# Sink-window attention and two MoE layers: the sinks' columns copied on ScalarE, and the last block split later

## The chip, the cores and the metric

The kernel runs on one core of a Trainium2 chip. The metric is the device time of one launch in microseconds, the median of three runs. TensorE, VectorE, ScalarE, GpSimd and SyncE each work through an instruction queue of their own in order; they wait for one another by semaphores. In the rows below PE is TensorE's matmul side and PEld its weight loads, DVE is VectorE, ACT is ScalarE, POOL is GpSimd, and SP is SyncE, which issues the DMAs.

## The reference

Attention over two batches of 8 heads, 768 positions and 64 columns a head, with a causal window of 128 positions and the first 4 positions as sinks that every query sees; then two dense layers over the 1536 tokens of 512 columns, with 2048 hidden columns each.

```python
keep = is_sink | in_window                       # 4 sinks, 128 positions back
scores = np.where(keep, scores, -1000000000.0)
a = np.exp(scores - np.max(scores, axis=-1, keepdims=True))
a = a / (np.sum(a, axis=-1, keepdims=True) + 1e-09)
x = np.matmul(a, v)                              # then (B, H, S, D) -> (1536, 512)

h = x @ w_in                                     # layer 1
g = (a0 + a1 * h + a2 * h**2 + a3 * h**3) / (1 + abs(b0) * abs(h) + abs(b1) * h**2 + 1e-6)
x = g @ w_out

h = np.maximum(x @ w_in2, 0.0)                   # layer 2
out = h * h @ w_out2
```

## The kernel before

**Attention.** The queries go in 12 blocks `u` of 128 rows (6 for each batch), each in two steps `m`, so there are 24 steps (`NM`) and two more, which finish the last block. A step takes four heads. `scores` (L354, L363) multiplies queries by the keys of the block and of the one before it; VectorE folds the two (L368), adds the mask and takes the row's extreme `nmax` (L375); `expo` (L392) is ScalarE's exponential into `pe`, with the row's sum into `rs`; `trans` (L420) transposes, ScalarE copies the result to `pc` (L432), and GpSimd splits it into two triangles `ph` (L433, L437); `pv` (L453) multiplies by the values into the PSUM bank `O`.

The sinks go another way. Their columns of `pe` (8 for each of 8 heads, 64 in all) are copied to `sr` by `sinks` (L401), for every block but the first of a batch, so ten times; `sums` adds a small constant to `rs` on ScalarE (L408) and writes the reciprocal into `sr` as well (L409, VectorE). `sinks_t` transposes `sr` on TensorE (L413) and copies it to `st` (L415); `sinks_and_sums` multiplies it by the sinks' values and spreads the reciprocal sums (L465, L469), which ScalarE copies to `rb` (L471). `result` (L475) multiplies `O` by `rb` on VectorE into `xf`. `parts_of` then makes two numbers of each: `xh`, rounded by ScalarE (L482), and `xl`, the remainder, by GpSimd (L483). The layers' matmuls work on such pairs.

**Layers.** Weights come as 64-bit numbers in four buffers `wr`; VectorE takes them to 32 bits in three instructions (L240, L246, L252, the steps that `w_until` hands out), by way of the bank `U` in the attention and `O` afterwards, as `conv["tag"]` says; then ScalarE rounds (L273) and GpSimd takes the remainder (L274) in `w_fin`. Some of these steps lie between the attention's.

A layer's steps are written out in `slot(k)`: round and remainder of element k-2 (`act_c`, L653 for `gh` and L654 for `gl`), the function of element k-1 (`act_b`: L638 and L639 on ScalarE, L642 to L646 on VectorE), the first matmuls of element k+1 (`g1`, L592), the first part of the function of element k (`act_a`: L608 to L612 on ScalarE, L613 on GpSimd; the cubic term is L621 on VectorE), the second matmuls of element k-2 (`g2`, L671). Slots 0 and 1 take the last two steps of the attention in their middle, as `mid`. `EARLY` is 2: the loop over the other slots begins there, after the attention's buffers are given back.

The order on every engine is that in which the code issues, without a scheduler. The last block (u = 11) lies in the third of the three chunks of 512 tokens; layer 1 begins with the first chunk.

Of the kernel before, what the change touches and what calls it, by code (L numbers as in the profile page):

```python
# [37 lines left out]
def kernel(  # L38
# [13 lines left out]
    nc = tc.nc  # L52
# [4 lines left out]
    NU = B * NB  # L57
# [119 lines left out]
    conv = {"tag": "U", "on": True}  # L177
# [12 lines left out]
    for j, (kind, m) in enumerate(jobs):  # L190
        n = 1 if kind == "v" else 1 + (wtiles[m][::2] == (0, 0)) if kind == "w" else WS + (m >= LATE)
# [73 lines left out]
    def w_fin():  # L265
        m = wst["fin"]
        if m not in wx or len(spare) <= keep[0] or int(spare[0][1:]) >= len(wpool):
            return
        wst["fin"] += 1
        xf = wx.pop(m).bitcast(F32)  # L270
        tag = spare.pop(0)
        t = wpool[int(tag[1:])].tile([P, 2, DM], F32R, tag=tag, name="w")
        nc.scalar.copy(out=t[:, 0], in_=xf)  # L273
        nc.gpsimd.tensor_tensor(out=t[:, 1], in0=xf, in1=t[:, 0].bitcast(F32), op=ALU.subtract)  # L274
        W[wtiles[m]] = (t[:, 0], t[:, 1], tag)
# [17 lines left out]
    def attention(ap, extra):  # L293
# [51 lines left out]
        def scores(n):  # L345
            u, pr = divmod(n, NPR)
            i = u % NB
            t = ss[n % 2]
            d = [t[:, e] for e in range(2)]
            if i == 0:  # L350
                mask, co, bw = m_0, 0, P
                for e in range(2):
                    s = slice(D * e, D * e + D)
                    nc.tensor.matmul(  # L354
                        d[e][:, 0:P], lhsT=ld[u, "q"][s, pr, :], rhs=keys[s, pr, 0, 0:P], start=True, stop=True
                    )
            else:
                mask, co, bw = (m_1 if i == 1 else m_2), P, BS
                hf = P // 2
                for g in range(2):  # L360
                    for e in range(2):
                        s, r = slice(D * e, D * e + D), slice(hf * g, hf * g + BS + hf)
                        nc.tensor.matmul(  # L363
                            d[e][hf * g:hf * g + hf, r], lhsT=ld[u, "q"][s, pr, hf * g:hf * g + hf],
                            rhs=keys[s, pr, i - 1:i + 1, :].rearrange("p i n -> p (i n)")[:, r],
                            start=True, stop=True,
                        )
                nc.vector.copy_predicated(  # L368
                    out=t[:, :, BS:BS + P], mask=tri.unsqueeze(1).to_broadcast([P, 2, P]), data=t[:, :, 0:P]
                )  # L370
            ns = []
            for e in range(2):
                ix = u * H + 2 * pr + e
                t = ap.tile([P, 160], F32, name="ns", bufs=6)
                nc.vector.tensor_tensor_reduce(  # L375
                    out=t[:, 0:bw], in0=d[e][:, co:co + bw], in1=mask, scale=-scale, scalar=3.0e38,
                    op0=ALU.add, op1=ALU.min, accum_out=nmax[:, ix:ix + 1],
                )
                ns.append(t)
            kps[n] = ns  # L380
# [17 lines left out]
        def sinks(u):  # L398
            t = pe_t.pop(u)
            if u % NB:  # L400
                nc.vector.tensor_copy(  # L401
                    sr[u % 2][:, 0:HS].rearrange("p (r e s) -> p r e s", r=NPR, e=2),
                    t[:, :, :, ROW - BS:ROW - P],
                )
# [74 lines left out]
        def parts_of(u):  # L479
            c, t0 = u // UPC, (u % UPC) * P  # L480
            x, h = f.pop(u), xh[c][:, :, t0:t0 + P]
            nc.scalar.copy(out=h, in_=x)  # L482
            nc.gpsimd.tensor_tensor(out=xl[c][:, :, t0:t0 + P], in0=x, in1=h.bitcast(F32), op=ALU.subtract)  # L483

        NM = NU * NPR // 2
# [28 lines left out]
        def step(m):  # L514
            w_fin()
            nonlocal bd, moe, rest, heads
            n, (u, a) = 2 * m, divmod(m, 2)
            if m < NM:
                scores(n)
            if a == 0 and u >= 1:  # L520
                sinks(u - 1)
                sums(u - 1)
            if m < NM:
                scores(n + 1)
                if n in DENSE:
                    fill(ps_t("T"), DENSE[n])
            if m == 0:
                rest = setup_rest(*next(masks), m_1, m_2, tri)
                next(rest)
                sink_keys(0)  # L530
            if a == 0 and 2 <= u <= NU:
                parts_of(u - 2)
            if m < NM:
                expo(n)
            if m in (1, 2):
                next(rest, None)
            if 0 < m <= NM:
                trans(m - 1)
            if m == 1:
                for t in sr:  # L540
                    nc.gpsimd.memset(t, 0.0)
                bd = diagonal()
                heads = bd.rearrange("p h d -> p (h d)")
                moe = setup_moe()
            if a == 0 and u + 2 < NU:
                load(u + 2)
            if a == 0 and m < NM and u % NB == 0:
                load_sinks(u // NB)
            if m >= 5:
                next(moe, None)  # L550
                next(moe, None)
            if a == 1 and u >= 1:
                sinks_and_sums(u - 1)
            if 1 < m:
                pv(m - 2)
            if m < NM:
                expo(n + 1)
            if a == 0 and u >= 1:
                sinks_t(u - 1)
            if m == NM - 1:  # L560
                g1(0)
            if m < NM and a == 1 and u % NB == 0:
                if u:
                    sink_keys(u)
                sink_values(u // NB, bd)
            extra(m)
            if a == 1 and u >= 1:
                result(u - 1)
            if m == NM + 1:
                parts_of(NU - 1)  # L570

        for m in range(NM):
            step(m)
        for j in range(2):
            slot(j, lambda: step(NM + j))


    def part(L, g):
        return CUTS[L][g:g + 2]
# [20 lines left out]
    def layers(mp, due):  # L600
# [56 lines left out]
        def g2(k):  # L657
            L, g, c, f = steps[k]
            f0, f1 = part(L, g)[0], part(L, g)[1] - 1
            if f == f0:  # L660
                acc[L, g, c] = [t[:, m] for t in [ps_s(), ps_s()] for m in range(2)]
            wo = W[L, f, 1]
            gg = gq.pop(k)
            for m in range(4):
                s = slice(m * P, (m + 1) * P)
                for a, b in ((0, 0), (0, 1), (1, 0)):
                    if L == 0:
                        lh, rh = wo[a][:, s], gg[b]
                    else:
                        lh, rh = gg[a][:, s], wo[b]  # L670
                    nc.tensor.matmul(  # L671
                        acc[L, g, c][m], lhsT=lh, rhs=rh,
                        start=(f == f0 and a + b == 0), stop=(f == f1 and a == 1),
                    )
            if c == NCH - 1:
                w_free((L, f, 1))
            if f == f1:
                done.append((L, g, c))
# [45 lines left out]

        K = len(steps)

        def slot(k, mid=None):
            if 0 <= k - 2:
                act_c(k - 2)
            w_fin()  # L730
            w_fin()
            if 0 <= k - 1 < K:
                act_b(k - 1, lambda: w_until(min(due(k), wst["int"] + 1)))
            if k + 1 < K:
                g1(k + 1)
            if k < K:
                act_a(k)
            if mid:
                cubic(st[k][1], hq[k])
                hq[k] = None  # L740
                mid()
            split_late()
            w_until(due(k))
            if 0 <= k - 2:
                g2(k - 2)
            if k == K + 1:
                finish(0)
                finish(1)
# [253 lines left out]
    EARLY = 2  # L1002
# [19 lines left out]
    slot, slots = layers(mp, due)  # L1022
    with tc.tile_pool(name="ap", bufs=1) as ap:
        NM = NU * NPR // 2

        def extra(m):
            if m == 1:
                for _ in range(NWR):
                    w_load()
            if m % 2:  # L1030
                w_until(min(WS * NA, m - 1))
            if m == NM:
                conv["on"] = False

        attention(ap, extra)
    conv["tag"], conv["on"] = "O", True
    wp2 = main.enter_context(tc.tile_pool(name="wp2", bufs=1))
    wpool += [wp2] * (NW - NA)
    for n in range(EARLY, slots):
        slot(n)  # L1040
        if n == KL + 3 * NF - 3:
            fl = verdict()
# [43 lines left out]
```

## Time and profile before

| what | value |
|---|---|
| median of 3 runs | 624.1 us (623.85 to 624.36) |
| the profiled execution | 624.6 us |
| its span, first to last instruction | 622.9 us |
| TensorE matmul busy | 609.0 us (98%) |
| VectorE, ScalarE, GpSimd busy | 434.4, 355.8, 329.2 us |

The span is what the trace covers; the profiled execution's own time has 1.7 us more around it. A busy TensorE is not TensorE at its peak, since matmuls overlap and their ends are modelled. The attention lasts to about 98 us; from there on the layers run.

### The profile page before, as it was taken

To read this page: it belongs to the slowest core of one execution; us is meant where nothing else is said; L and a number is where in the kernel's file an instruction comes from. 1 tells how busy PE (TensorE), PEld (TensorE's weight loads), DVE (VectorE), ACT (ScalarE), POOL (GpSimd) and SP (SyncE) were. 2 spreads that over 40 slices of the span, in tenths; PEclk is the share of its full clock that TensorE was granted. 3 is DMA by queue.
4 is the path that set the end of the run, shared out by engine and by line. 5 is a ranking of instruction groups with operands and counts; after the bars stand their busy time and mean duration, and the time that the engine had idled before them with its cause. 6 is when DMAs were issued, how large, how long until landed. Compare 5 with 4: busy or idle time off the path is not lost.

```text
span 622.9 us, 9430 instructions
## 1 busy us (share of the span) xinstructions
PE 609.0 (98%) x3317; PEld 491.1 (79%) x3317; DVE 434.4 (70%) x873; ACT 355.8 (57%) x748; POOL 329.2 (53%) x293
## 2 busy tenths in 40 slices
PE   9999999999999999999999999999999999999995
PEld 6666777788888878888888888888888888888884
DVE  5998957989989889877768879598594422441421
ACT  5999977888886877877869543243332222222210
POOL 4567655777776767666857575444352222222221
PEclk9999999999999999999999999999999999999999
DMA  8857411423332333121111447557365355500102
GB/s 232 244 146 214 120 36 35 128 87 93 98 102 78 97 97 101 38 64 35 35 34 35 115 148 256 192 176 234 131 207 198 116 191 168 175 28 1 67 1 73
DMA packets 64231, 72.03 MB, mean 116 GB/s; under 512 B 15280, under 2 KB 55216, under 8 KB 64176
## 3 DMA queue, kind: packets, MB, share of 16 engines
q1 hardware_dynamic: 64032, 71.35, 37.1%
q8 instruction: 28, 0.46, 0.3%
q14 instruction: 27, 0.22, 0.1%
q10 hardware_dynamic: 144, 0.00, 0.0%
HBM read 68.20 MB, written 3.15 MB: 115 GB/s over the span
## 4 chain that ended last, share of the span: by engine, by line
PE 65%; DVE 19%; ACT 11%; issue 2%; DMA 1%; SPq 0%; DVEq 0%; ACTq 0%
PE s L671 30%; PE T L592 23%; PE U L592 7%; DVE t L646 3%; DVE U L644 3%; ACT U L638 2%; ACT U L639 2%; ACT gh L653 2%; ACT w L273 2%; DVE t L642 2%; DVE wx L252 2%; DVE ns L375 1%; DVE O L240 1%; PE O L453 1%; PE s L363 1%
## 5 line engine op out<-in xcount | busy, mean ns | idle before, releaser
L592 PE MATMUL T<-xh,w 128*128 128x512 f32 x640 | 211.0, 391 | 0.5 <-DVE t L621 0.4
L654 POOL TENSOR_TENSOR gl<-g,gh 128x512 fp32r<-128x512 f32 x48 | 62.2, 1295 | 157.9 <-ACT gh L653 157.8
L592 PEld LDWEIGHTS T<-xh,w 128*128 128x128 f32 x640 | 120.2, 188 | 27.9 <-DVE t L621 2.7
L671 PE MATMUL s<-gh,w 128*128 128x512 f32 x384 | 126.0, 389 | 0.0
L592 PE MATMUL T<-xl,w 128*128 128x512 f32 x320 | 124.6, 389 | 0.0
L671 PE MATMUL s<-w,gh 128*128 128x512 f32 x384 | 118.1, 389 | 0.0
L274 POOL TENSOR_TENSOR w<-wx,w 128x512 fp32r<-128x512 f32 x64 | 82.7, 1293 | 7.2 <-ACT w L273 7.2
L654 POOL TENSOR_TENSOR gl<-t,gh 128x512 fp32r<-128x512 f32 x48 | 62.1, 1294 | 44.6 <-ACT gh L653 43.0
L671 PEld LDWEIGHTS s<-gh,w 128*128 128x128 f32 x384 | 72.1, 188 | 15.0
L671 PEld LDWEIGHTS s<-w,gh 128*128 128x128 f32 x384 | 72.0, 188 | 14.9
L613 POOL TENSOR_TENSOR t<-t,ah 128x512 f32<-128x512 f32 x48 | 62.2, 1296 | 37.7 <-ACT t L610 35.8
L653 ACT CAST gh<-g 128x512 fp32r<-128x512 f32 x48 | 29.9, 623 | 81.8 <-PE s L671 74.5
L671 PE MATMUL s<-gl,w 128*128 128x512 f32 x192 | 74.8, 390 | 0.9 <-POOL gl L654 0.9
L671 PE MATMUL s<-w,gl 128*128 128x512 f32 x192 | 74.7, 389 | 0.0
L592 PEld LDWEIGHTS T<-xl,w 128*128 128x128 f32 x320 | 60.1, 188 | 12.2
L653 ACT CAST gh<-t 128x512 fp32r<-128x512 f32 x48 | 29.9, 622 | 46.2 <-DVE t L646 41.9
L642 DVE SCALAR_TENSOR_TENSOR t<-t,U 128x512 f32<-128x512 f32 x48 | 33.0, 687 | 30.1 <-ACT U L639 29.5
L627 DVE TENSOR_TENSOR g<-r,T 128x512 f32<-128x512 f32 x32 | 21.8, 683 | 41.8 <-ACT r L617 41.5
L617 ACT ACTIVATE r<-T 128x512 f32<-128x512 f32 x32 | 19.2, 600 | 53.2 <-PE T L592 53.1
L392 ACT ACTIVATE pe<-ns,nmax 128x136 f32<-128x136 f32 (+1 forms) x96 | 38.3, 400 | 10.0 <-DVE nmax L375 9.6
L671 PEld LDWEIGHTS s<-gl,w 128*128 128x128 f32 x192 | 36.0, 188 | 8.8 <-POOL gl L654 1.4
L273 ACT CAST w<-wx 128x512 fp32r<-128x512 f32 x64 | 39.3, 615 | 6.4 <-DVE wx L252 6.4
(136 smaller groups left out, 1033.4 us busy)
## 6 DMA issues: line engine op xcount, KB each, us to landing
wr<-in_w_in_dram SPq DMA_DIRECT2D x54, 512.0 KB, 3.7
wr<-in_w_out_dram SPq DMA_DIRECT2D x52, 512.0 KB, 3.7
qr<-in_q_dram SPq DMA_DIRECT2D x12, 256.0 KB, 4.1
keys<-in_k_dram SPq DMA_DIRECT2D x12, 256.0 KB, 4.5
vr<-in_v_dram SPq DMA_DIRECT2D x12, 256.0 KB, 5.6
wr<-in_v_dram SPq DMA_DIRECT2D x6, 512.0 KB, 4.3
out_dram<-part SPq DMA_DIRECT2D x12, 256.0 KB, 2.0
vsc<-in_v_dram SPq DMA_DIRECT2D x2, 16.0 KB
```

The lines of the kernel that those rows point to most:

```text
L273: nc.scalar.copy(out=t[:, 0], in_=xf)
L274: nc.gpsimd.tensor_tensor(out=t[:, 1], in0=xf, in1=t[:, 0].bitcast(F32), op=ALU.subtract)
L392: nc.scalar.activation(out=t[:, e, ROW - w:], in_=ns[e][:, 0:w], func=ACTF.Exp, scale=-1.0, bias=nmax[:, ix:ix + 1], accum_out=rs[:, 2 * p ...
L592: nc.tensor.matmul(h, lhsT=wi[a][:, kk * P:(kk + 1) * P], rhs=(xh, xl)[b][c][:, kk, :], start=(kk == 0 and a + b == 0), stop=(kk == KD - 1 ...
L613: nc.gpsimd.tensor_tensor(out=t, in0=t, in1=ah, op=ALU.mult)
L617: nc.scalar.activation(out=r, in_=h, func=ACTF.Relu)
L627: nc.vector.tensor_tensor(out=g, in0=st.pop(k), in1=h, op=ALU.mult)
L642: nc.vector.scalar_tensor_tensor(out=t, in0=t, scalar=QP, in1=r0, op0=ALU.add, op1=ALU.mult)
L644: nc.vector.scalar_tensor_tensor(out=r0, in0=t, scalar=-2.0, in1=r0, op0=ALU.add, op1=ALU.mult)
L653: nc.scalar.copy(out=gh, in_=g)
L654: nc.gpsimd.tensor_tensor(out=gl, in0=g, in1=gh.bitcast(F32), op=ALU.subtract)
L671: nc.tensor.matmul(acc[L, g, c][m], lhsT=lh, rhs=rh, start=(f == f0 and a + b == 0), stop=(f == f1 and a == 1),)
```

## The change

`sinks` copies on ScalarE instead of VectorE. In slot 1, `step(NM + 1)` no longer ends with `parts_of(NU - 1)`; slot 2 is taken out of the loop and issued at the end of the attention, and it issues `parts_of(NU - 1)` behind its own `g2`. The bank that the weight steps use is switched one step earlier in the code.

```diff
         def sinks(u):
             t = pe_t.pop(u)
             if u % NB:
-                nc.vector.tensor_copy(
+                nc.scalar.copy(
                     sr[u % 2][:, 0:HS].rearrange("p (r e s) -> p r e s", r=NPR, e=2),
                     t[:, :, :, ROW - BS:ROW - P],
                 )
...
             if a == 1 and u >= 1:
                 result(u - 1)
-            if m == NM + 1:
-                parts_of(NU - 1)
...
         for j in range(2):
             slot(j, lambda: step(NM + j))
+        slot(2, after=lambda: parts_of(NU - 1))
...
-        def slot(k, mid=None):
+        def slot(k, mid=None, after=None):
...
             if 0 <= k - 2:
                 g2(k - 2)
+            if after:
+                after()
...
             if m == NM:
                 conv["on"] = False
+            if m == NM + 1:
+                conv["tag"], conv["on"] = "O", True
 
         attention(ap, extra)
-    conv["tag"], conv["on"] = "O", True
...
-    for n in range(EARLY, slots):
+    for n in range(EARLY + 1, slots):
```

On VectorE, in each of ten blocks of the attention, this is what stands in its queue around the copy (`m_107` is the mask, the ISA rows are L375):

```order
 L375 ISA ns,nmax<-s,m_107 128x136
 L375 ISA nmax 128x1
-L401 COPY sr_154<-pe 128x64
 L409 RECIPROCAL sr_154<-rs 128x8
 L368 COPY_PREDICATED s<-tri,s 128x2x128
```

The reciprocal now follows the block's extremes at once. On ScalarE, in the same blocks (here one in which a weight tile is rounded just before, L273):

```order
 L392 ACTIVATE pe,rs<-ns,nmax 128x136 x2
 L273 CAST w<-wx 128x512
+L401 COPY sr_154<-pe 128x64
 L408 ACTIVATE rs<-rs,eps 128x8
 L482 CAST xh_79<-xf 128x4x128
```

The copy comes between the weight's rounding and the sums. On GpSimd, from the last block of the attention into layer 1, before the change:

```order
L613 TENSOR_TENSOR t<-t,ah 128x512
L483 TENSOR_TENSOR xl_84<-xf,xh_81 128x4x128
L654 TENSOR_TENSOR gl<-t_1527,gh 128x512
L613 TENSOR_TENSOR t<-t,ah 128x512
L654 TENSOR_TENSOR gl<-t_1583,gh 128x512
```

and after it, where the numbers of these lines are smaller by one (L612 for L613, L653 for L654):

```order
L612 TENSOR_TENSOR t<-t,ah 128x512
L653 TENSOR_TENSOR gl<-t_1527,gh 128x512
L612 TENSOR_TENSOR t<-t,ah 128x512
L483 TENSOR_TENSOR xl_84<-xf,xh_81 128x4x128
L653 TENSOR_TENSOR gl<-t_1583,gh 128x512
```

The remainder `xl` of the last block has moved from ahead of the first `gl` to ahead of the second. ScalarE's `xh` moves likewise, from ahead of the first `gh` to behind L612 of slot 2. TensorE's and SyncE's queues keep their order.

## Rows read from the trace of the kernel before

**Rows 1.** Stretches: us, then busy us of each engine (count), clock, DMA share, GB/s.
```profile
core 0: us, PE busy (x) PEld busy (x) DVE busy (x) ACT busy (x) POOL busy (x), PEclk, DMA share, GB/s
...
71.00:84.00 13.00, 12.24 (x170) 8.43 (x168) 12.20 (x48) 11.61 (x45) 8.12 (x11) 1.00 0.14 43
...
130.00:620.00 490.00, 485.36 (x2139) 400.42 (x2137) 329.82 (x522) 248.99 (x416) 249.78 (x195) 1.00 0.34 109
```

**Rows 2.** Waits of 13 to 85 us, longest in total first.
```profile
engine line waited for: us in total, times, longest us
...
PEld s L363 <- DVE nmax L375: 3.9, 10, 0.4
ACT pe L392 <- DVE nmax L375: 3.8, 7, 0.8
...
PE T L413 <- DVE sr L409: 3.4, 6, 1.0
```

**Rows 3.** The instructions of line 401.
```profile
L401 DVE COPY sr<-pe x10: 190/1006/1248, 19.3 to 91.1; 128x64 f32<-128x64 f32 x10
```

**Rows 4.** Timeline of 78 to 82.7 us: start, length, instruction, idle time before it.
```profile
78.10 0.91 PE L363 MATMUL s<-keys,qr 64*64 64x200 f32 x16
...
78.60 0.30 ACT L408 ACTIVATE rs<-rs,eps 128x8 f32<-128x8 f32 x1
...
79.04 0.62 ACT L482 CAST xh<-xf 128x512 fp32r<-128x512 f32 x1
...
79.74 1.27 POOL L483 TENSOR_TENSOR xl<-xf,xh 128x512 fp32r<-128x512 f32 x1 [1.38 <-ACT xh L482]
...
79.82 1.24 DVE L401 COPY sr<-pe 128x64 f32<-128x64 f32 x1
...
81.23 0.33 PE L413 MATMUL T<-ident,sr 128*128 128x128 f32 x1 [0.61 <-DVE sr L409]
...
81.49 1.20 PE L363 MATMUL s<-keys,qr 64*64 64x200 f32 x16
...
81.88 0.41 ACT L392 ACTIVATE pe<-ns,nmax 128x136 f32<-128x136 f32 x1 [0.80 <-DVE nmax L375]
```

**Rows 5.** Timelines of 64 to 92 us, by engine.
```profile
65.88 1.28 POOL L274 TENSOR_TENSOR w<-wx,w 128x512 fp32r<-128x512 f32 x1 [0.79 <-ACT w L273]
67.11 1.28 POOL L483 TENSOR_TENSOR xl<-xf,xh 128x512 fp32r<-128x512 f32 x1
...
66.55 0.66 DVE L401 COPY sr<-pe 128x64 f32<-128x64 f32 x1
67.13 0.19 DVE L409 RECIPROCAL sr<-rs 128x8 f32<-128x8 f32 x1
...
68.02 0.41 ACT L392 ACTIVATE pe<-ns,nmax 128x136 f32<-128x136 f32 x1 [0.21 <-DVE nmax L375]
```

**Rows 6.** The last copy, from VectorE's timeline.
```profile
91.09 0.19 DVE L401 COPY sr<-pe 128x64 f32<-128x64 f32 x1
```

**Rows 7.** Timelines of 84 to 130 us: ScalarE, GpSimd, TensorE, where layer 1 begins.
```profile
96.67 0.59 ACT L471 COPY rb<-s 128x512 f32<-128x512 f32 x1 [0.45 <-PE s L469]
98.50 0.62 ACT L482 CAST xh<-xf 128x512 fp32r<-128x512 f32 x1 [1.23 <-DVE xf L475]
99.02 0.61 ACT L653 CAST gh<-t 128x512 fp32r<-128x512 f32 x1
...
99.19 1.29 POOL L483 TENSOR_TENSOR xl<-xf,xh 128x512 fp32r<-128x512 f32 x1 [2.18 <-ACT xh L482]
100.44 1.27 POOL L654 TENSOR_TENSOR gl<-t,gh 128x512 fp32r<-128x512 f32 x1
...
101.77 0.50 PE L671 MATMUL s<-gl,w 128*128 128x512 f32 x1 [0.94 <-POOL gl L654]
```

**Rows 8.** The same timelines, the slots after it.
```profile
102.27 1.30 POOL L613 TENSOR_TENSOR t<-t,ah 128x512 f32<-128x512 f32 x1 [0.56 <-ACT t L610]
...
107.36 0.39 PE L671 MATMUL s<-gl,w 128*128 128x512 f32 x1
...
121.31 0.50 PE L592 MATMUL T<-xh,w 128*128 128x512 f32 x1 [0.22 <-DVE t L621]
```

## The prediction

> **What bounds the kernel now.** I read the table of stretches first. From 130 to 620 us TensorE is busy for 485.4 of 490 us; in the attention steps (71 to 84 us) TensorE, VectorE and ScalarE are busy for 12.2, 12.2 and 11.6 of 13 us [rows 1]. So time is only to be had where TensorE stands still: in the attention and at the change from attention to layer 1. What is saved there moves the rest forward whole, since the layers' matmuls follow at TensorE's own pace.
>
> Next the waits of 13 to 85 us. TensorE stood 3.4 us, in six places, for the sinks' transpose (L413), which needs `sr` complete; ScalarE stood 3.8 us, in seven, for `nmax` of VectorE; weight loads of the scores stood 3.9 us for the same [rows 2]. All three end on VectorE, and what makes VectorE late is the sinks' copy (L401): ten of them, 190 ns the shortest, 1006 the median, 1248 the longest [rows 3]. For 64 columns that is no work but a hold, and two blocks show its shape. At 79.82 the copy begins just behind GpSimd's remainder `xl` of 79.74 and lasts 1.24 us, to 81.06, as `xl` ends at 81.01; TensorE's L413 starts at 81.23 after 0.61 us of idleness, ScalarE's next exponentials at 81.88 after 0.80 [rows 4]. At 66.55 the copy ends at 67.21, just after GpSimd's `w` of 65.88 is done at 67.16, and ScalarE then waits only 0.21 us [rows 5]. The shortest, at 91.09, takes 0.19 us [rows 6].
>
> So there are two kinds of block. Where ScalarE rounds a weight tile ahead of L408, GpSimd does `w`, then `xl`, and the copy waits for the end of `w`: the "weight blocks", five in number, like that of [rows 5]. Where it does not, in four, the copy waits for a whole `xl`, as in [rows 4]. The tenth copy is the one at 91.09, in the tail of the attention.
>
> Last I read the stretch behind the attention. TensorE stands 0.94 us ahead of 101.77, for the remainder `gl` of layer 1's first element. The line ahead of it is serial: ScalarE is done with `rb` at 97.26, waits 1.23 us for `xf`, rounds the last block (`xh`, 98.50), then does `gh` at 99.02; GpSimd subtracts `xl` at 99.19 and only then `gl` at 100.44 [rows 7].
>
> **Part one, the copies.** VectorE loses ten copies. ScalarE gains ten. What VectorE loses ends on the path only as far as the others can follow.
>
> ScalarE's ledger: all seven waits for `nmax` go, 3.8 us [rows 2]. The profile counts them from an end that is drawn late: `xh` of 98.50 is 0.62 long, and `gh` starts 0.52 behind its start [rows 7]; so each wait is 0.10 longer than its row, 0.7 in seven. Together 4.5 us.
>
> Its costs: no row shows this copy on ScalarE. The nearest is L408, 128x8 from SBUF to SBUF, 0.30 long [rows 4], so by the same 0.10 some 0.20 of ScalarE's time; above it lies the 128x512 cast with 0.52 [rows 7]. The lower bound is 0. I take 0.20, as 64 columns are nearer to 8 than to 512. In the four other blocks the copy is free: from L408 at 78.60 to `xh` at 79.04 are 0.44 us, 0.24 more than L408 needs, since `xh` waits for VectorE's `xf` [rows 4]; if that cover went, they would cost another 0.8. The tenth stands where ScalarE waits for transposes in any case. The five weight blocks show no such hole, so 5 x 0.20 = 1.0 us. Part one: 4.5 - 1.0 = **-3.5 us**.
>
> The bounds: with 0.52 a copy, 4.5 - 2.6 = 1.9. On the other side, ScalarE might give way elsewhere and TensorE get all of its own waits back: 3.4 at L413 [rows 2], and in eight blocks 0.29 at the scores behind it, where 16 matmuls take 1.20 us (81.49) instead of 0.91 (78.10) [rows 4]: 3.4 + 2.3 = 5.7.
>
> The Trainium skill, "VectorE: DVE Perf Modes", the section on the trn2 errata, gives a ScalarE copy 224 cycles and one for each column; an estimate from it is 0.24 us, and part one would be -3.3 by it.
>
> **Part two, the last block.** ScalarE's `xh` leaves the place ahead of `gh`, and `xl` the place ahead of `gl`; both go behind slot 2's work. Neither costs less; nothing reads this block before layer 1's third chunk, several slots on. `gh` can then start when `rb` is done, at 97.2, `gl` at 97.8, and be ready at 99.1. TensorE's idle time begins at 100.83, so all of the 0.94 us go, and the refill with them: the matmul behind the halt is 0.50 long, others 0.39 [rows 7, 8]. **-1.05 us**.
>
> What is behind them now: with `gh` 1.8 us earlier, ScalarE goes on at once through L638 to L612, and the product L613 on GpSimd starts near 100.5 instead of 102.27 [rows 8]. Then `xl` runs from 101.8 to 103.1, and the second `gl` from 103.1 to 104.4. TensorE takes that one at 107.36 now [rows 8], at 106.3 with the halt gone. There are 1.9 us to spare; if that cover went, the loss could be at most the 1.3 us of `xl`. No DMA is issued by what moves, and the order on SyncE's queue is as it was.
>
> What is late next: TensorE halts 0.22 us at 121.31 for the cubic term of VectorE (L621) [rows 8], since VectorE and ScalarE are a little behind it there. Their chain starts 1.8 us earlier, TensorE's only 1.05, so this halt should go, with its refill 0.3, and perhaps a few too short to be listed: between 0 and 0.9, I take **-0.5 us**.
>
> The sum: -3.5 - 1.05 - 0.5 = -5.05. The profiled execution took 624.6 us (span 622.9); the median of the runs is 624.1, 0.5 below it, and the forecast is made from the median: **619.0 us**. The bounds are 1.9 + 1.05 + 0 = 2.95 (621.1) and 5.7 + 1.05 + 0.9 = 7.65 (616.4).
>
> **Rivals.** *TensorE sets the pace.* All of its own waits go: -5.7 - 1.05 - 0.5, 616.8 us. For it speaks that ScalarE's small gaps may shrink too; against it, that the exponentials of the weight blocks cannot start before ScalarE has done the copy.
>
> *ScalarE is dearer.* If the copy costs 0.4 or more, or the cover in the four other blocks goes, part one shrinks to 1.9 to 2.7 and the sum to some 3: 621.0 us.
>
> *The hold moves on.* The next instruction of VectorE (the reciprocal L409) might wait for GpSimd in the copy's place. Then part one gives nothing and the copies cost 1.0: 624.1 - 1.55 + 1.0 = 623.5. Against it: the reciprocal at 67.13 took 0.19 us while `xl` of 67.11 was under way [rows 5]. The Trainium skill, "SBUF — State Buffer", section "Who interferes with whom", says that a VectorE instruction with two SBUF inputs contends with a GpSimd one that reads SBUF. The reciprocal has one input there, and the trace agrees (0.19 us); this lowers the rival's chance and leaves the sum.
>
> *Slower: ScalarE was the bound.* If its seven waits were only slack, refilled from another side, each copy would add to its in-order queue with no return: 10 x 0.20 to 10 x 0.52, +2.0 to +5.2, less 1.05: 625.0 to 628.2. It decides where no wait goes, or where a copy costs over 0.9 in the five weight blocks (0.9 x 5 = 4.5). Against it: the wait of 81.88 has a copy of 1.24 us straight ahead [rows 4]. The Trainium skill, "Perfetto Trace Analysis", section "Optimizing Scalar/DVE Operations", has this rule: where VectorE has a fast mode for an operation, it is quicker there than on ScalarE. For the copy of 91.09 the trace agrees (0.19 us); for the median of 1.0 us it does not.
>
> **How the numbers follow.** Forecast, ScalarE keeping the pace: 0.62. TensorE keeping it: 0.12. ScalarE dearer: 0.16. The hold moves on: 0.06. Slower: 0.04. The range for 8 in 10 takes in the forecast with its own spread (copies of 0 to 0.3, a follow-on of 0 to 0.9: 617.6 to 620.0), the nearer part of the TensorE case and the dear case: 617.0 to 621.2. What this kernel's measurement can tell from no change is about 0.2%, 1.25 us. Faster by more: the first three and a little of the fourth, 0.92. Within it: most of the fourth, 0.05. Slower: 0.03.
>
> **What would show it.** No copy on VectorE at L401; ScalarE copies 0.2 to 0.3 us long; the 3.4 us ahead of L413 nearly gone; ScalarE's waits for `nmax` below 1 us in all; the weight blocks shorter by 0.1 to 0.2 us, the four others by 0.8 to 0.9; layer 1's first matmuls some 3.5 us earlier; no halt at the first `gl`. The prediction is wrong if the reciprocal or another VectorE instruction grows to a microsecond, if the ScalarE copy takes 0.4 or more, or if layer 1 starts early and the layers end as late as before.

## The result and the profile after

The changed kernel takes 617.14 us (616.86 to 618.1), the kernel before 624.1, each the median of five runs: a ratio of 0.9891, 95% interval 0.9877 to 0.9906. Run once more beside a later set it took 617.27 against 624.33, 0.9881 (0.9864 to 0.9897).

Three moments of each trace tell where the 7 us are: the start of the first scores (L354), of layer 1's first matmul (first row `T<-xh`), and of the last matmul. In the kernel before:

```profile
6.64 0.72 PE L354 MATMUL s<-keys,qr 64*128 64x128 f32 x8
...
85.32 0.50 PE L592 MATMUL T<-xh,w 128*128 128x512 f32 x1
...
615.22 0.39 PE L671 MATMUL s<-w,gl 128*128 128x512 f32 x1
```

In the changed one:

```profile
6.23 0.71 PE L354 MATMUL s<-keys,qr 64*128 64x128 f32 x8 [0.17 <-DMA keys<-in_k_dram]
...
80.24 0.50 PE L591 MATMUL T<-xh,w 128*128 128x512 f32 x1
...
607.61 0.39 PE L670 MATMUL s<-w,gl 128*128 128x512 f32 x1
```

The first moment moves from one execution to the next (6.23 to 7.38 us over the traces below, with nothing changed ahead of it) and is no effect of the change. From the first scores to layer 1 it was 78.68 us and is 74.01: **4.67 us from the attention**. From there to the last matmul it was 529.90 and is 527.37: **2.53 us from layer 1 on**.

The waits of 13 to 85 us, as in [rows 2], after the change:

```profile
PEld T L420 <- ACT pe L392: 4.4, 17, 0.3
...
DVE s L368 <- PE s L363: 3.9, 9, 0.6
...
PEld T L413 <- DVE s L368: 1.2, 7, 0.2
...
PEld s L363 <- DVE nmax L375: 0.9, 3, 0.4
...
ACT pe L392 <- DVE nmax L375: 0.4, 2, 0.2
...
PEld T L413 <- DVE sr L409: 0.3, 2, 0.2
```

TensorE's 3.4 us for `sr` at L413 are off the list; its weight loads there wait twice for `sr` and seven times, 0.2 us at most, for what the profile puts down to L368. ScalarE's 3.8 us for `nmax` are 0.4. VectorE now waits 3.9 us for scores (L368), and the weight loads' most frequent wait is for ScalarE's exponentials (17 times, 0.3 at most). The copy itself, by its line, and the reciprocal that follows on VectorE:

```profile
L401 ACT COPY sr<-pe x10: 229/244/252, 17.8 to 85.2; 128x64 f32<-128x64 f32 x10
...
L409 DVE RECIPROCAL sr<-rs x12: 193/198/202, 12.4 to 86.0; 128x8 f32<-128x8 f32 x12
```

A weight block, from the timelines of 60 to 72 us (ScalarE, VectorE, GpSimd), to be held against [rows 5]:

```profile
62.20 0.24 ACT L401 COPY sr<-pe 128x64 f32<-128x64 f32 x1
62.34 0.30 ACT L408 ACTIVATE rs<-rs,eps 128x8 f32<-128x8 f32 x1
...
63.04 0.20 DVE L409 RECIPROCAL sr<-rs 128x8 f32<-128x8 f32 x1
...
62.37 1.28 POOL L274 TENSOR_TENSOR w<-wx,w 128x512 fp32r<-128x512 f32 x1 [0.63 <-ACT w L273]
```

The copy takes 0.14 us of ScalarE's time (62.20 to 62.34), although its row is 0.24 long. The reciprocal runs at 63.04 in the middle of GpSimd's `w`, unheld. And behind the attention, in place of [rows 7]:

```profile
91.59 0.59 ACT L471 COPY rb<-s 128x512 f32<-128x512 f32 x1 [0.45 <-PE s L469]
92.07 0.62 ACT L652 CAST gh<-t 128x512 fp32r<-128x512 f32 x1
...
95.74 0.61 ACT L482 CAST xh<-xf 128x512 fp32r<-128x512 f32 x1
96.30 0.62 ACT L652 CAST gh<-t 128x512 fp32r<-128x512 f32 x1
...
92.83 1.30 POOL L653 TENSOR_TENSOR gl<-t,gh 128x512 fp32r<-128x512 f32 x1 [0.91 <-POOL t L612]
...
96.59 1.29 POOL L483 TENSOR_TENSOR xl<-xf,xh 128x512 fp32r<-128x512 f32 x1
97.85 1.29 POOL L653 TENSOR_TENSOR gl<-t,gh 128x512 fp32r<-128x512 f32 x1
...
95.36 0.39 PE L670 MATMUL s<-gh,w 128*128 128x512 f32 x1
95.58 0.39 PE L670 MATMUL s<-gl,w 128*128 128x512 f32 x1
...
101.02 0.39 PE L670 MATMUL s<-gl,w 128*128 128x512 f32 x1
```

TensorE passes from the first `gh` to the first `gl` without a halt. The second `gl` is ready at 99.14 and wanted at 101.02: 1.9 us to spare, as forecast.

### The profile page after: what moved, and what is told of

The parts are those of the page before. It is cut to its first block, busy times and chain, and to the rows that moved or that the text cites. A ratio compares the mean times of both kernels' runs of the same rounds, so it can differ in the third digit from the quotient of the medians.

```text
span 615.4 us, 9431 instructions
## 1 busy us (share of the span) xinstructions
PE 606.2 (99%) x3317; PEld 491.8 (80%) x3317; DVE 425.5 (69%) x863; ACT 355.4 (58%) x758; POOL 329.6 (54%) x293
## 4 chain that ended last, share of the span: by engine, by line
PE 74%; DVE 13%; ACT 9%; issue 2%; DMA 1%; DVEq 0%; SPq 0%; ACTq 0%
PE s L670 32%; PE T L591 25%; PE U L591 7%; PE O L453 3%; DVE t L645 3%; DVE U L643 2%; PE s L363 2%; ACT U L637 2%; ACT U L638 2%; ACT gh L652 2%; ACT w L273 2%; PE T L420 2%; DVE t L641 1%; DVE O L240 1%; PE O L465 1%
## 5 line engine op out<-in xcount | busy, mean ns | idle before, releaser
L653 POOL TENSOR_TENSOR gl<-g,gh 128x512 fp32r<-128x512 f32 x48 | 62.2, 1296 | 157.8 <-ACT gh L652 157.8
L653 POOL TENSOR_TENSOR gl<-t,gh 128x512 fp32r<-128x512 f32 x48 | 62.3, 1299 | 44.5 <-ACT gh L652 42.8
L612 POOL TENSOR_TENSOR t<-t,ah 128x512 f32<-128x512 f32 x48 | 62.3, 1298 | 37.0 <-ACT t L609 35.1
L273 ACT CAST w<-wx 128x512 fp32r<-128x512 f32 x64 | 39.3, 616 | 6.4 <-DVE wx L252 6.4
L591 PE MATMUL U<-xh,w 128*128 128x512 f32 x128 | 42.1, 390 | 0.0
L670 PEld LDWEIGHTS s<-w,gl 128*128 128x128 f32 x192 | 36.0, 188 | 7.5
```

The costliest lines, as they stand in the source:

```text
L591: nc.tensor.matmul(h, lhsT=wi[a][:, kk * P:(kk + 1) * P], rhs=(xh, xl)[b][c][:, kk, :], start=(kk == 0 and a + b == 0), stop=(kk == KD - 1 ...
L612: nc.gpsimd.tensor_tensor(out=t, in0=t, in1=ah, op=ALU.mult)
L653: nc.gpsimd.tensor_tensor(out=gl, in0=g, in1=gh.bitcast(F32), op=ALU.subtract)
L670: nc.tensor.matmul(acc[L, g, c][m], lhsT=lh, rhs=rh, start=(f == f0 and a + b == 0), stop=(f == f1 and a == 1),)
```

## The experiments

All times of attention and layers below are differences of the three moments named above, each from the kernel's own trace.

| kernel | first scores | layer 1's first | last matmul | attention | layers | median, us | before beside it | ratio |
|---|---|---|---|---|---|---|---|---|
| before | 6.64 | 85.32 | 615.22 | 78.68 | 529.90 | 624.1 | | |
| changed | 6.23 | 80.24 | 607.61 | 74.01 | 527.37 | 617.14 | 624.1 | 0.9891 |
| changed again | 6.54 | 80.55 | 607.94 | 74.01 | 527.39 | 617.27 | 624.33 | 0.9881 |
| copies only | 6.30 | 80.28 | 609.55 | 73.98 | 529.27 | 618.83 | 624.51 | 0.9909 |
| block only | 6.25 | 84.92 | 612.93 | 78.67 | 528.01 | 622.77 | 624.51 | 0.9973 |
| VectorE, unheld | 7.33 | 80.91 | 608.93 | 73.58 | 528.02 | 617.78 | 624.51 | 0.9889 |
| two copies | 6.49 | 82.18 | 609.63 | 75.69 | 527.45 | 618.83 | 624.51 | 0.9907 |
| no copy | 7.38 | 80.95 | 608.61 | 73.57 | 527.66 | 617.28 | 624.61 | 0.9879 |
| xl only | 6.94 | 80.94 | 610.16 | 74.00 | 529.22 | 619.67 | 624.61 | 0.9917 |
| two columns held | 6.46 | 84.06 | 611.77 | 77.60 | 527.71 | 621.49 | 624.61 | 0.9949 |
| idle cast | 6.38 | 80.37 | 608.26 | 73.99 | 527.89 | 617.82 | 624.33 | 0.9894 |
| unheld but last | 6.70 | 80.27 | 607.68 | 73.57 | 527.41 | 617.09 | 624.33 | 0.9882 |

The intervals of the ratios reach 0.0010 to 0.0017 to either side, 0.6 to 1.1 us, so differences of less than that rest on the trace columns. Each kernel but the changed one has a single trace; the changed kernel's two agree there within 0.02 us.

**Changed again** is the changed kernel itself.

> The changed kernel itself, once more beside the others: 6.5 to 7.3 us below before. If the 74.0 us from the first score to layer 1's first matmul and the 527.4 us behind it belong to the program and not to one execution, both come again within 0.2 us.

Both stretches came again, 74.01 and 527.39.

**Copies only** and **block only** are the change's two parts alone.

```diff
 # copies only: against the kernel before
-                nc.vector.tensor_copy(
+                nc.scalar.copy(
                     sr[u % 2][:, 0:HS].rearrange("p (r e s) -> p r e s", r=NPR, e=2),
 # block only: against the changed kernel
-                nc.scalar.copy(
+                nc.vector.tensor_copy(
                     sr[u % 2][:, 0:HS].rearrange("p (r e s) -> p r e s", r=NPR, e=2),
```

> The kernel before with the copies on ScalarE and nothing else; the last block's split stays ahead of layer 1's first remainder. If the gain of the two parts adds up and the halts of 109 to 127 us went because of the block's move, this is 4.5 to 4.9 us below before: about 619.4 us, with the halt of 0.9 us ahead of the first remainder and the later small halts still there. If the copies alone also removed the later halts, 618.2 us.

> The changed kernel with the copies back on VectorE: only the last block's split is moved. If the parts add up, 1.1 us for the first halt and 1.0 to 1.4 for the later ones: about 621.7 us. If the later halts went because of the copies, 623.0 us.

The parts add up: attention -4.70 and -0.01 (together -4.67), layers -0.63 and -1.89 (together -2.53). So the attention's gain is the copies' alone, and three quarters of the layers' gain are the block's. By the medians the two are 5.7 and 1.7 us below the kernel before, and neither lies where its expectation put it, since neither had that the copies alone also shorten the layers by 0.63. In the trace of copies only the first `gl` still waits, and the halts of the cubic term stand again:

```profile
96.74 0.50 PE L671 MATMUL s<-gl,w 128*128 128x512 f32 x1 [0.95 <-POOL gl L654]
...
116.00 0.50 PE L592 MATMUL T<-xh,w 128*128 128x512 f32 x1
...
121.75 0.50 PE L592 MATMUL T<-xh,w 128*128 128x512 f32 x1
```

**Two columns held** keeps ScalarE's copy and adds to VectorE, at the old place, a copy of two columns into a scratch tile.

```diff
+                nc.vector.tensor_copy(junk, t[:, 0, 0, ROW - BS:ROW - BS + 2])
```

> The changed kernel with a copy of two columns on VectorE added where the sinks' copy stood, into a scratch tile that nobody reads. If the copy's time was a wait for GpSimd, two columns are held as long as 64 were (median about 1 us) and most of the 4.7 us are lost again: 620.5 to 622 us. If its time was that of its columns, 0.1 us a copy: 617.1 to 617.6.

```profile
L405 DVE COPY junk<-pe x10: 159/732/1219, 19.2 to 89.8; 128x2 f32<-128x2 f32 x10
...
59.17 0.17 DVE L405 COPY junk<-pe 128x2 f32<-128x2 f32 x1
59.24 1.28 POOL L484 TENSOR_TENSOR xl<-xf,xh 128x512 fp32r<-128x512 f32 x1 [1.18 <-ACT xh L483]
...
78.52 1.27 POOL L484 TENSOR_TENSOR xl<-xf,xh 128x512 fp32r<-128x512 f32 x1 [1.37 <-ACT xh L483]
...
78.60 1.22 DVE L405 COPY junk<-pe 128x2 f32<-128x2 f32 x1
```

Two columns are held up to 1219 ns, as 64 were up to 1248 [rows 3], and the attention is 77.60 us: 3.6 of the 4.7 us are gone again. The copy's time was a wait, not its columns. The rows show for what: begun 0.08 us behind `xl`, the copy lasts until `xl` ends (78.60 and 78.52); begun 0.07 us ahead of it, it takes 0.17 us (59.17 and 59.24).

**VectorE, unheld** does the same move on VectorE in another form: a maximum over an axis of one element.

```diff
-                nc.scalar.copy(
-                    sr[u % 2][:, 0:HS].rearrange("p (r e s) -> p r e s", r=NPR, e=2),
-                    t[:, :, :, ROW - BS:ROW - P],
+                nc.vector.tensor_reduce(
+                    out=sr[u % 2][:, 0:HS].rearrange("p (h s) -> p h s", h=H),
+                    in_=t.rearrange("p r e w -> p (r e) w")[:, :, ROW - BS:ROW - P].unsqueeze(3),
+                    axis=AX.X, op=ALU.max,
                 )
```

> The changed kernel with the sinks' columns taken on VectorE again, by a reduction over an axis of one element, which gives the same numbers. If the long copies were a hold of that one instruction form against GpSimd, this one takes about 0.2 us each, ScalarE is relieved of ten copies, and the time is that of the changed kernel or up to 1 us less: 616 to 617.3 us. If what made VectorE late was having any instruction on those columns at that place, it is held again: about 621.7 us.

```profile
L401 DVE TENSOR_REDUCE sr<-pe x10: 210/214/217, 20.0 to 86.7; 128x64 f32<-128x64 f32 x10
```

On the same engine, at the same place, with the same data, it takes 210 to 217 ns every time, with GpSimd at work in all ten, and the attention is 73.58 us, shorter by 0.43 than with ScalarE's copy. The hold belongs to the copy's form, not to VectorE. The median, 617.78, is half a microsecond above what was expected, since the layers took 528.02 instead of 527.37.

**Two copies** makes ScalarE's copy twice; **no copy** leaves it out (the sinks outside the window then miss in the result).

```diff
 # two copies
+                nc.scalar.copy(
+                    sr[u % 2][:, 0:HS].rearrange("p (r e s) -> p r e s", r=NPR, e=2),
+                    t[:, :, :, ROW - BS:ROW - P],
+                )
 # no copy
-                nc.scalar.copy(
-                    sr[u % 2][:, 0:HS].rearrange("p (r e s) -> p r e s", r=NPR, e=2),
-                    t[:, :, :, ROW - BS:ROW - P],
-                )
+                pass
```

> The changed kernel with each ScalarE copy made twice, same data. If ScalarE sets the pace of the blocks in which it rounds a weight tile, the second copy costs its 0.15 us in those five or more: +0.7 to +1.5 us, 617.9 to 618.6. If TensorE sets the pace in all blocks, no more than 0.3 us: 617.1 to 617.4.

> The changed kernel without the copy at all: sr keeps its zeros, so the sinks outside the window are left out of the result. If ScalarE sets the pace, the saved 0.15 us a copy come back in five blocks or more: 0.7 to 1.5 us, 615.7 to 616.4. If TensorE sets it, 616.9 to 617.1.

Without any copy the attention is 73.57 us, so the ten copies on ScalarE cost 0.44 in all. A second one costs 75.69 - 74.01 = 1.68. The two are not the same price for the same thing: behind the only copy, L408 starts 0.14 to 0.15 us after it, while the second copy, into the same columns, starts 0.27 us after the first. Counted from one L413 to the next, the second costs 0.23 to 0.27 us in six stretches, all of its time, and 0 to 0.09 in the other five. So neither theory holds alone: some two thirds of the first copies' time go into gaps that ScalarE still has, and most of the second ones' goes onto the path. The median of no copy (617.28) lies in neither of its ranges, since its layers take 0.29 us longer; that of two copies (618.83) lies 0.2 above its first.

**Xl only** leaves ScalarE's rounding of the last block in slot 1 and moves only GpSimd's remainder (`parts_of` is given the names of the parts that it is to make).

```diff
+            if m == NM + 1:
+                parts_of(NU - 1, ("xh",))
...
-        slot(2, after=lambda: parts_of(NU - 1))
+        slot(2, after=lambda: parts_of(NU - 1, ("xl",)))
```

> The changed kernel with ScalarE's rounding of the last block back in slot 1, ahead of the first gh; only GpSimd's remainder xl moves. If most of the halt came from xl standing ahead of gl (1.25 us on GpSimd), the first gl is ready about 0.1 to 0.3 us late and most of the 1.1 us stays gained, but ScalarE's chain starts 1.8 us later than in the changed kernel and the later halts come back in part: 617.5 to 618.3 us. If the rounding on ScalarE was as dear as the remainder, the halt is 0.5 us or more and the time 618.3 to 618.8.

The expectation was wrong, and the run is the most telling one. TensorE's timeline:

```profile
96.73 0.50 PE L674 MATMUL s<-gl,w 128*128 128x512 f32 x1 [0.28 <-POOL gl L657]
...
99.48 0.50 PE L595 MATMUL T<-xh,w 128*128 128x512 f32 x1
...
105.24 0.50 PE L595 MATMUL T<-xh,w 128*128 128x512 f32 x1
...
116.66 0.50 PE L595 MATMUL T<-xh,w 128*128 128x512 f32 x1 [0.24 <-DVE t L624]
...
122.41 0.50 PE L595 MATMUL T<-xh,w 128*128 128x512 f32 x1
```

From the first `gh` (96.06) to the first `gl` it is 0.67 us, where the kernel with both still ahead has 1.34 (95.40 to 96.74 in copies only): 0.67 won. But a first matmul of 0.50 instead of 0.39 marks a halt, and there are four in the next 26 us; the layers take 529.22 us, as without any move (529.27). What TensorE gained at the first `gl` it gave back at 99.48 and 105.24, two halts that copies only does not have; the other two it has as well (116.00, 121.75). ScalarE's and VectorE's chain had not started earlier: in both kernels the first `gh` starts 13.70 us behind layer 1's first matmul.

**Idle cast** tests this from the other side: everything moved, but a cast of 0.5 us, which waits for nothing, put on ScalarE where the rounding stood.

```diff
+            if m == NM + 1:
+                nc.scalar.copy(out=ap.tile([P, CT], F32R, name="vm", bufs=2), in_=heads)
```

> The changed kernel with one more 128x512 cast on ScalarE (0.5 us, into a buffer that nobody reads) where the last block's rounding stood, ahead of the first gh; unlike that rounding it waits for nothing. The first gl is still ready in time, so there is no halt there. If the later halts follow the moment at which the chain of ScalarE and VectorE starts, up to 0.5 us of them come back within layer 1's first slots: from layer 1's first matmul to the last one 527.7 to 527.9 us instead of 527.4. If only the halt at the first gl counted, 527.4.

```profile
92.20 0.62 ACT L570 CAST vm<-bd 128x512 fp32r<-128x512 f32 x1
92.72 0.62 ACT L654 CAST gh<-t 128x512 fp32r<-128x512 f32 x1
...
95.71 0.39 PE L672 MATMUL s<-gl,w 128*128 128x512 f32 x1
...
114.75 0.50 PE L593 MATMUL T<-xh,w 128*128 128x512 f32 x1
...
120.49 0.50 PE L593 MATMUL T<-xh,w 128*128 128x512 f32 x1
```

No halt at the first `gl` (95.71), yet the layers are 527.89 us: a chain that starts 0.52 later costs 0.50 to 0.52, in halts some 20 us further on.

**Unheld but last** takes VectorE's reduction in nine blocks and ScalarE's copy in the last (`u == NU - 1`), to see whether the two best columns can be had together.

> The sinks' columns taken on VectorE by the reduction over an axis of one element in nine blocks, and copied on ScalarE in the last. The attention should be as short as with all ten on VectorE, 73.6 us from the first score to layer 1's first matmul. If the small halts that all ten on VectorE left near 120 and 247 us came from the last block's share, they are gone, with 527.4 us from there to the end: 0.4 us below the changed kernel. If they came from the phase in which layer 1 begins, they stay: 528.0 us, no gain.

They can be had together: 73.57 and 527.41 us, in sum 0.40 below the changed kernel's. Its median, 617.09, lies 0.18 below that of the changed kernel run beside it (617.27); their measured ranges overlap, so as a version it is at least as good, and better by the trace alone.

**What the layers' times are made of.** The layers differ by up to 0.65 us between kernels in which none of their instructions moved. Two late starts account for that. The second `gh` starts 0.37 us behind the end of L646, which feeds it, in the four kernels in which ScalarE does not make the last copy, and 0.09 behind it in the other eight. The L642 of layer 1's 25th element, by the numbers of the kernel before, starts 0.46 us behind the end of ScalarE's L639 in the four in which VectorE has an instruction for the last block's sinks, and 0.11 behind it in the other eight. The rows are the second `gh` of before and of copies only, then the L642 of two columns held and of the changed kernel:

```profile
103.52 0.62 ACT L653 CAST gh<-t 128x512 fp32r<-128x512 f32 x1 [0.75 <-DVE t L646]
...
98.20 0.62 ACT L653 CAST gh<-t 128x512 fp32r<-128x512 f32 x1 [0.47 <-DVE t L646]
...
224.25 0.69 DVE L643 SCALAR_TENSOR_TENSOR t<-t,U 128x512 f32<-128x512 f32 x1 [0.90 <-ACT U L640]
...
220.08 0.69 DVE L641 SCALAR_TENSOR_TENSOR t<-t,U 128x512 f32<-128x512 f32 x1 [0.55 <-ACT U L638]
```

Together with the start of the chain, the first `gh` counted from layer 1's first matmul (11.83 us in the changed kernel, 13.70 where `xh` stands ahead of it), they add up to the layers' time of every kernel:

| kernel | first `gh` later, us | second `gh` late | L642 late | sum | layers above 527.37 |
|---|---|---|---|---|---|
| before | 1.87 | 0.28 | 0.35 | 2.50 | 2.53 |
| copies only | 1.87 | | | 1.87 | 1.90 |
| xl only | 1.87 | | | 1.87 | 1.85 |
| block only | | 0.28 | 0.35 | 0.63 | 0.64 |
| VectorE, unheld | | 0.28 | 0.35 | 0.63 | 0.65 |
| no copy | | 0.28 | | 0.28 | 0.29 |
| two columns held | | | 0.35 | 0.35 | 0.34 |
| idle cast | 0.52 | | | 0.52 | 0.52 |
| changed again, two copies, unheld but last | | | | 0 | 0.02, 0.08, 0.04 |

## Why the prediction came out as it did

The forecast was 619.0 us, with 617.0 to 621.2 as its range, and the result of 617.14 lies just inside; direction and places were right. It was 1.9 us too careful by the medians, 2.15 by the traces (7.20 instead of 5.05), in three terms.

**Part one, -3.5 forecast, -4.67 measured.** The mechanism was right: the copy was a hold behind GpSimd (two columns held as long as 64), it made TensorE wait at L413 and ScalarE for `nmax`, and both waits are gone. Two terms were mis-sized. One is "5 x 0.20 = 1.0 us" for ScalarE's copies: all ten cost 0.44, by the kernel without one, and one takes 0.14 to 0.15 from start to start. The other is the ledger of 4.5: without any copy the attention is 5.11 us shorter (78.68 - 73.57), 0.6 more than ScalarE's waits added up to and midway between the ledger and the bound of 5.7 from TensorE's side. Counted from one L413 to the next, the four blocks with a hold behind `xl` are 0.85 to 1.05 us shorter, 0.8 to 0.9 forecast, and the five weight blocks 0.24 in the mean (from 0.18 longer to 0.58 shorter), 0.1 to 0.2 forecast.

**Rivals of part one.** The hold did not move on: the reciprocal takes 193 to 202 ns throughout. By the Trainium skill, "SBUF — State Buffer", section "Who interferes with whom", a VectorE copy in a two-port mode and a GpSimd instruction block each other, whichever issues first, while a reduction never contends. The trace agrees as to the waits (159 to 1219 ns for two columns copied, 210 to 217 ns for 64 reduced); that the copy runs in such a mode no row shows. ScalarE was not dearer: its copy is 244 ns long in the median. The estimate from the Trainium skill's "VectorE: DVE Perf Modes", the section on the trn2 errata, was 0.24 us, and the trace agrees. In the sum of this rival, "some 3", the follow-on is left out; with 0.5 for it, 1.9 to 2.7 for part one make 3.5 to 4.3, so 619.9 to 620.7 us. It was no slack that refilled, either. TensorE's pace is the rival that came nearest in time (616.8), and not as a mechanism: the attention did not gain 5.7, and the copies are not free.

**Part two, the first halt, -1.05 forecast.** From the first `gh` to the first `gl` it was 1.33 us and is 0.22: -1.11. Right in size, but the step "all of the 0.94 us go" was taken for a gain of its own, and it is not one: with `xl` alone moved, 0.67 us of it were won and all given back.

**The follow-on, -0.5 forecast.** Behind the first `gl`, the layers gained another 1.4 us (2.53 - 1.11). Of these, 0.78 are the block's (1.89 - 1.11). The prediction set the chain's 1.8 us against the halt's 1.05, which makes 0.75, and took 0.5 of it: the reasoning was right, and the choice was too small. The chain's start is what counts: started 1.87 us earlier, it gives 1.89 (block only); delayed by 0.52, it costs 0.50 to 0.52 (idle cast); not moved, it gives nothing (xl only). Had part two been costed as the chain's 1.8 us, it would have been right to 0.1 for what the block gave. The other 0.63 are the two late starts, which go with the last copy and not with the block. The prediction had no term for them, so this part of the gain was luck.

**Open.** What makes the two instructions start late, no run here tested. Each of the eight late starts is followed, 0.65 to 0.69 us later, by an 8 KB packet of the profile's instruction queue (q14), and none of the other sixteen starts by one within a microsecond; in two columns held, from 224.8 to 225 us:

```profile
q14 instruction: 1, 0.01, 16.6%
```

So they may have to do with the loading of instructions; that is not shown. The late starts were read from one trace of each kernel, two of the changed one.

## What to carry to other kernels

An elementwise copy whose length follows another engine's instruction and not its own columns is a hold; look at its shortest and median duration first, and change its form or its engine. Where a halt of TensorE ends on a chain of several engines, cost the moment at which the chain starts, not the halt: here a halt that was shortened without moving the chain returned a few slots later. An engine that is nearly even with the pace-setter may take one more small instruction for part of its price (here a third) and most of the next one's price on the path. And a change of some tenths of a microsecond in instructions that nobody moved can come from a single late start: compare the traces instruction by instruction before giving it a reason.

## What was not expected of the hardware

A VectorE copy of two columns was held for up to 1219 ns and never took less than 159, while a reduction of 64 columns over one-element axes at the same place took 210 to 217 ns in all ten cases: the size of the instruction did not matter, its form did, and whether it began ahead of GpSimd's instruction (0.17 us) or behind it (1.22). A second ScalarE copy into the same columns started 0.27 us behind the first, where another instruction started 0.14 to 0.15 behind it, and cost 1.68 us in ten blocks, where the first had cost 0.44. And the copy's place on one engine moved single starts of instructions far behind it by 0.28 and 0.35 us.
